# Query and key transposes moved from TensorE to the crossbar DMA from batch 3 on, with earlier loads, in a fused attention and mixer kernel

## The chip, the cores and the metric

One core of one Trainium2 chip. The metric is the device time of one execution in microseconds (us), lower is better. Times of one kernel on one chip mostly lie within 1%, with some executions over 1.5% above the fastest; those are called slow and left out of ratios, though not out of the medians. A ratio is the mean time of one kernel's fast runs over the mean of the kernel before's fast runs in the same rounds on the same chip, so it is not quite the ratio of the medians quoted beside it. The kernel before has medians from 400.4 to 406.0 us in the different rounds, so only ratios compare across rounds.

## The reference, cut to what matters

```python
# attention: B, H, S, D = 8, 8, 576, 64; q, k, v are 0.1 * randn, s is 0.5 * randn
scores = (1 / sqrt(D)) * q @ k.T                      # per head
cum    = cumsum(maximum(s, 0))
scores = where(causal, -1e9, scores + minimum(-(cum[:, None] - cum[None, :]), 0))
attn   = softmax(scores) @ v
# mixer on x = attention, heads side by side: [8, 576, 512]
u   = x + (x.T @ U @ V).T                             # rank 32, along the sequence
out = u + maximum(u @ w_ch1, 0) @ w_ch2               # 512 -> 2048 -> 512
```

## The kernel before: the parts that matter

The kernel works in pairs of heads: 32 pairs, four to a batch, numbered `n`. For a pair it needs q and k with the head dimension on the partitions ("slot"), and gets them by TensorE transposes into PSUM (the memory that TensorE's results land in) and VectorE copies out of it. Between the steps of attention (`run`), each `yield` lets a piece of the channel mixer (`fill`, four matmuls of 512 columns) go onto TensorE.

```python
def transposes(n):                       # pair n of batch b
    slot = slots[n % NSLOT]              # five slots
    ...                                  # rows of cum into the slot, by DMA
    for hh in range(2):
        tp = pwork()...                  # PSUM
        for c, src in enumerate((q_t[b], k_t[b])):
            for t2 in range(4):
                nc.tensor.transpose(tp[:, c, t2, :], src[:, h, ds(t2 * 128, 128)], identity[:TP, :TP])
        for par in range(2):
            copy(dst[:, :, :, :, par], tp[par * D : par * D + D]...)   # VectorE
        yield
...
load(2)
...
for n in range(PB, NP + 2):              # the second stage, pairs 4 to 31
    b, hp = divmod(n, PB)
    if hp == 0 and 1 < b < B - 1:
        load(b + 1)                      # q, k and v of the next batch, on GpSimd's queue
    if n + 1 < NP: run(transposes(n + 1))
    if n < NP:     run(scores(n))
    if hp == 1 and b > FT:
        run(seqmix(b - 1)); fill.append(chanmix(b - 1))
    if PB < n <= NP: run(values(n - 1))
    ...
in_program_order(tc, traced, [E.Pool, E.PE])
```

`values` ends in a VectorE division (a reciprocal and a multiply into `x_sb`) and a crossbar DMA (a DMA that transposes on its way) of `x_sb` into `xT`, which `seqmix` adds when it writes `uT`. The last line: in the second stage only GpSimd and TensorE run in the order of the program. The instructions of VectorE, ScalarE and SyncE are put in an order by the build tool, by when it expects each to be ready. VectorE then starts them in the order of its list: in the changed kernel below it sits idle 11.60 us in front of a copy while a reciprocal waits behind it.

The softmax here doesn't subtract the row's maximum and nothing guards it: scores larger than these inputs give would overflow.

## Time and profile before

| | before |
|---|---|
| median, first three runs | 404.92 us (401.1 to 407.01) |
| profiled execution | 403.4 us span, TensorE busy 95% |
| TensorE idle in a steady batch (182 to 223 us) | 0.28 of 41 us |
| period of a steady batch | 41.2 us |

The lines are in the prediction below. A line of the timeline gives start and duration in us, engine (PE is TensorE, DVE VectorE, ACT ScalarE, POOL GpSimd, SPq SyncE's queue), line of the program, operation, tile written and tile read, and in brackets the idle time before it and what ended that. A window row gives the busy us of each engine in that stretch. The period of a batch is the distance between the first matmuls of successive channel mixers (L442), which stand in the chain of waits at 184.22, 225.40 and 266.60 us.

### The profile page before, as it was taken

To read this page: it belongs to the slowest core of one execution; us is meant where nothing else is said; L and a number is where in the kernel's file an instruction comes from. 1 tells how busy PE (TensorE), PEld (TensorE's weight loads), DVE (VectorE), ACT (ScalarE), POOL (GpSimd) and SP (SyncE) were. 2 spreads that over 40 slices of the span, in tenths; PEclk is the share of its full clock that TensorE was granted. 3 is DMA by queue.
4 is the path that set the end of the run, shared out by engine and by line. 5 is a ranking of instruction groups with operands and counts; after the bars stand their busy time and mean duration, and the time that the engine had idled before them with its cause. 6 is when DMAs were issued, how large, how long until landed. Compare 5 with 4: busy or idle time off the path is not lost.

```text
span 403.4 us, 8541 instructions
## 1 busy us (share of the span) xinstructions
PE 382.8 (95%) x3525; PEld 218.2 (54%) x3525; DVE 223.3 (55%) x484; ACT 201.0 (50%) x384; POOL 56.3 (14%) x79
## 2 busy tenths in 40 slices
PE   7798998798999999999999999999999999999995
PEld 3575445465555556655555565555565554444442
DVE  7875124587756775667566856785678353002011
ACT  5552479551874358534853386328642930530710
POOL 5750023320230041003200230000000000000000
PEclk9758999999999999999999999999999999999999
DMA  5999999999399359837992599251224014301002
GB/s 76 169 211 207 151 93 102 134 151 105 61 153 111 73 97 137 79 72 112 147 80 72 100 151 70 63 122 21 19 70 120 18 34 130 80 18 69 19 26 79
DMA packets 94149, 38.33 MB, mean 95 GB/s; under 512 B 77150, under 2 KB 88446, under 8 KB 94110
## 3 DMA queue, kind: packets, MB, share of 16 engines
q0 software_dynamic: 53360, 18.44, 59.8%
q1 hardware_dynamic: 40750, 19.35, 26.7%
q8 instruction: 27, 0.44, 0.5%
q14 instruction: 12, 0.10, 0.1%
HBM read 37.51 MB, written 9.95 MB: 118 GB/s over the span
## 4 chain that ended last, share of the span: by engine, by line
PE 82%; DMA 10%; DVE 5%; POOL 1%; issue 1%; ACT 1%; DVEq 0%; ACTq 0%
PE pwork L454 29%; PE pwork L442 29%; PE pscore L260 10%; DMA k_sd<-in_k_dram 7%; PE pwork L323 6%; PE pwork L239 3%; DMA v_slot_102<-in_v_dram 2%; DVE o_sb L464 1%; PE pscore L151 1%; PE pwork L395 1%; DVE x_sb L333 1%; PE pwork L352 1%; DMA hT<-in_s_dram 1%; POOL v_slot_102 L193 1%; ACT pT_87 L271 0%
## 5 line engine op out<-in xcount | busy, mean ns | idle before, releaser
L454 PE MATMUL pwork<-w_sb,hT 128*128 128x512 bf16 x576 | 142.2, 381 | 0.2 <-ACT slot_96 L245 0.2
L442 PE MATMUL pwork<-uT,w_sb 128*128 128x512 bf16 x576 | 141.0, 379 | 0.6 <-ACT slot_96 L245 0.3
L449 ACT ACTIVATE hT<-pwork 128x512 bf16<-128x512 f32 x144 | 87.8, 609 | 107.7 <-PE pwork L442 107.1
L454 PEld LDWEIGHTS <-hT 128*128 128x128 bf16 x576 | 51.8, 98 | 49.1 <-issue 0.8
L442 PEld LDWEIGHTS <-w_sb 128*128 128x128 bf16 x576 | 50.6, 98 | 47.4 <-DVE uT L377 0.7
L464 DVE TENSOR_TENSOR o_sb<-pwork,u_sd 128x512 f32<-128x512 f32 x36 | 24.9, 692 | 63.8 <-PE pwork L454 62.6
L271 ACT ACTIVATE pT_87<-pscore 128x512 bf16<-128x512 f32 x32 | 19.3, 603 | 30.7 <-PE pscore L260 30.6
L333 DVE TENSOR_TENSOR x_sb<-pwork,rec 128x320 bf16<-128x320 f32 x64 | 31.3, 490 | 2.0
L271 ACT ACTIVATE pT_86<-pscore 128x512 bf16<-128x512 f32 x32 | 19.3, 603 | 19.5 <-PE pscore L260 19.4
L99 POOL DMA_DIRECT2D q_sd<-in_q_dram x10 | 8.1, 811 | 142.1 <-PE pwork L239 126.6
L245 DVE COPY slot_96<-pwork 64x576 bf16<-64x576 bf16 x22 | 17.4, 797 | 13.9 <-PE pwork L239 13.6
L272 DVE TENSOR_TENSOR pT_87<-pT_87,keep 128x512 bf16<-128x512 bf16 x32 | 13.2, 416 | 20.5 <-ACT pT_87 L271 20.5
L272 DVE TENSOR_TENSOR pT_86<-pT_86,keep 128x512 bf16<-128x512 bf16 x32 | 13.2, 414 | 18.5 <-ACT pT_86 L271 18.4
L239 PEld LDWEIGHTS <-q_sd 72*128 72x128 bf16 x256 | 16.3, 100 | 13.2 <-DMA q_sd<-in_q_dram 1.3
L239 PE MATMUL pwork<-identity,k_sd 72*128 72x72 bf16 x256 | 19.2, 201 | 4.2 <-DMA k_sd<-in_k_dram 4.2
L377 DVE TENSOR_TENSOR uT<-pwork,xT 128x256 bf16<-128x256 f32 (+6 forms) x54 | 19.4, 418 | 6.4 <-PE pwork L395 6.4
L323 PEld LDWEIGHTS <-pT_86 128*128 128x128 bf16 x480 | 19.0, 100 | 7.2 <-issue 2.0
L332 DVE RECIPROCAL rec<-pwork 128x5 f32<-128x5 f32 x64 | 12.2, 192 | 19.2 <-PE pwork L323 18.9
L284 ACT ACTIVATE pT_87<-pscore 128x512 bf16<-128x512 f32 x32 | 19.5, 610 | 6.2 <-PE pscore L260 6.2
L284 ACT ACTIVATE pT_86<-pscore 128x512 bf16<-128x512 f32 x32 | 19.5, 611 | 4.7 <-PE pscore L260 4.6
L245 DVE COPY slot_93<-pwork 64x576 bf16<-64x576 bf16 x26 | 20.6, 796 | 2.0 <-PE pwork L239 1.6
L323 PEld LDWEIGHTS <-pT_87 128*128 128x128 bf16 x480 | 18.8, 100 | 5.3 <-DVE pT_87 L297 0.3
(100 smaller groups left out, 441.3 us busy)
## 6 DMA issues: line engine op xcount, KB each, us to landing
out_dram<-o_sb SPq DMA_DIRECT2D x36, 256.0 KB
w_sb<-in_moe_w_ch_dram POOLq DMA_DIRECT2D x2, 2048.0 KB, 20.8
q_sd<-in_q_dram POOLq DMA_DIRECT2D x7, 576.0 KB, 8.4
k_sd<-in_k_dram POOLq DMA_DIRECT2D x7, 576.0 KB, 14.0
v_slot_102<-in_v_dram POOLq DMA_DIRECT2D x12, 128.0 KB, 13.5
v_slot_103<-in_v_dram POOLq DMA_DIRECT2D x12, 128.0 KB, 15.3
v_slot_104<-in_v_dram POOLq DMA_DIRECT2D x8, 128.0 KB, 17.6
rows_hbm<-hT SPq DMA_DIRECT2D x1, 504.0 KB
```

The lines of the kernel that those rows point to most:

```text
L239: nc.tensor.transpose(tp[:, c, t2, :], src[:, h, ds(t2 * 128, 128)], identity[:TP, :TP])
L245: copy(dst[:, :, :, :, par], tp[par * D : par * D + D].rearrange("p c t m -> p c m t"),)
L260: nc.tensor.matmul(dst, lhsT=kT[:, ds(j * 128, 128)], rhs=qT[:, lo:hi], start=True, stop=True,)
L271: nc.scalar.activation(pT[:, hh, 0:512], diag, EXP, scale=scale)
L272: nc.vector.tensor_tensor(pT[:, hh, 0:512].rearrange("p (a b) -> p a b", a=4), pT[:, hh, 0:512].rearrange("p (a b) -> p a b", a=4), keep.t ...
L284: nc.scalar.activation(pT[:, hh, 512:1024], far, EXP, scale=scale)
L323: nc.tensor.matmul(po[:, i, :], lhsT=pT[:, hh, ds(place(j, i), 128)], rhs=vt[:, j, h, :], start=(j == 0), stop=(j == i), skip_group_check= ...
L333: nc.vector.tensor_tensor(x_sb[:, hp, :, ds(hh * D, D)], po[:, :, 0:D], rec.to_broadcast([128, 5, D]), op=ALU.mult,)
L442: nc.tensor.matmul(f1, lhsT=w1_sb[:, kt, ds(nf * 128, 128)], rhs=u[:, kt, :], start=(kt == 0), stop=(kt == 3),)
L449: nc.scalar.activation(hT[:, nf, :], f1, RELU)
L454: nc.tensor.matmul(f2, lhsT=hT[:, nf, ds(i * 128, 128)], rhs=w2_sb[:, nf, :], start=(nf == 0), stop=(nf == NF - 1),)
L464: nc.vector.tensor_tensor(o_sb.rearrange("p (a b) -> p a b", a=4), f2.rearrange("p (a b) -> p a b", a=4), u_sd[:, :, i, :], op=ALU.add,)
```

## The change

Its intent: take 320 transposes off TensorE, which bounds the kernel, and let the DMA crossbar do them from batch 3 on, three pairs ahead. The q and k buffers become one tensor of 80 rows of which 72 are data, because the number of rows has to be a multiple of 16 (the prediction names the page); the spare eight are filled once by a DMA. The loads of q and k move two batches ahead.

```diff
+    qks = [consts.tile([TR, H, 2, TT * D], BF16, name=f"qk{i}") for i in range(2)]     # TR = 80
+    def fetch(n):
+        qkT_of[n] = work.tile([128, 2, 2, 4, TR], BF16, tag="qkT", name="qkT", bufs=3)
+        nc.sync.dma_start_transpose(out=qkT_of[n]..., in_=qks[b % 2][:, ds(2 * hp, 2), :, :]...)
     def transposes(n):
+        qkT = qkT_of.pop(n, None)
+            if qkT is not None:
+                tp = qkT[:, hh, :, :, :TP]           # the copies then read SBUF
+            else: ...                                # TensorE, as before
-        uxT = work.tile(..., tag="uxT")              # also ux
+        uxT = work.tile(..., tag="uxT", bufs=1)
...
-            load(b + 1)
+            load_v(b + 1)
+        nb = b + 2
+        if hp == (1 if b >= QT else 3) and QT <= nb < B:      # QT = 3
+            load_qk(nb, 0, H)
+        if hp == 1 and QT - 2 <= b < QT:
+            nc.sync.dma_start(out=qks[b % 2][TP:], in_=qks[b % 2][2 * TP - TR : TP])
+        if QT * PB <= n + 3 < NP:
+            fetch(n + 3)
```

More of the change, by code (lines that the diff above doesn't have):

```diff
@@ L70 @@
     FT = 2
+    QT = 3
     consts = ctx.enter_context(tc.tile_pool(name="consts", bufs=1))
-    loads = ctx.enter_context(tc.tile_pool(name="loads", bufs=2))
     work = ctx.enter_context(tc.tile_pool(name="work", bufs=2))
@@ L89 @@
     nc.sync.dma_start(out=s_sb, in_=s.rearrange("b h s -> (b h) s"))
-    q_t, k_t = {}, {}
-    def alloc_qk(b):
-        q_t[b] = loads.tile([TP, H, TT * D], BF16, tag="q_sd", name="q_sd")
-        k_t[b] = loads.tile([TP, H, TT * D], BF16, tag="k_sd", name="k_sd")
+    TR = 80
+    qks = [consts.tile([TR, H, 2, TT * D], BF16, name=f"qk{i}") for i in range(2)]
     def load_qk(b, h, n):
-        for dst, src in ((q_t[b], q), (k_t[b], k)):
+        for c, src in enumerate((q, k)):
             nc.gpsimd.dma_start(
-                out=dst[:, ds(h, n), :],
+                out=qks[b % 2][:TP, ds(h, n), c, :],
                 in_=src[b, ds(h, n)].rearrange("h (p t) d -> p h (t d)", p=TP),
             )
-    alloc_qk(0)
     load_qk(0, 0, 2)
@@ L169 @@
             )
-    for dst in (q_t[0], k_t[0]):
-        nc.vector.memset(dst[:, 4:8, 0:2], 0.0)
+    nc.vector.memset(qks[0][:TP, 4:8, :, 0:2], 0.0)
     load_qk(0, 4, 4)
@@ L210 @@
     nc.gpsimd.dma_start(out=w2_sb, in_=moe_w_ch2.rearrange("(kt kp) n -> kp kt n", kp=128))
-    alloc_qk(1)
     load_qk(1, 0, H)
     load_v(1)
-    uT_of, x_of, xT_of = {}, {}, {}
+    uT_of, x_of, xT_of, qkT_of = {}, {}, {}, {}
     def uT(g):
@@ L220, in uT @@
         return uT_of[g]
+    def fetch(n):
+        b, hp = divmod(n, PB)
+        qkT_of[n] = work.tile([128, 2, 2, 4, TR], BF16, tag="qkT", name="qkT", bufs=3)
+        nc.sync.dma_start_transpose(
+            out=qkT_of[n].rearrange("p a c t m -> p (a c t) m"),
+            in_=qks[b % 2][:, ds(2 * hp, 2), :, :].rearrange("p h c x -> p (h c x)"),
+        )
     def transposes(n):
@@ L231, in transposes @@
             )
+        qkT = qkT_of.pop(n, None)
         for hh in range(2):
             h = 2 * hp + hh
-            tp = pwork().bitcast(BF16)[:, : 2 * 4 * TP].rearrange(
-                "p (c t m) -> p c t m", c=2, t=4
-            )
-            for c, src in enumerate((q_t[b], k_t[b])):
-                for t2 in range(4):
-                    nc.tensor.transpose(
-                        tp[:, c, t2, :], src[:, h, ds(t2 * 128, 128)], identity[:TP, :TP]
-                    )
+            if qkT is not None:
+                tp = qkT[:, hh, :, :, :TP]
+            else:
+                tp = pwork().bitcast(BF16)[:, : 2 * 4 * TP].rearrange(
+                    "p (c t m) -> p c t m", c=2, t=4
+                )
+                for c in range(2):
+                    for t2 in range(4):
+                        nc.tensor.transpose(
+                            tp[:, c, t2, :],
+                            qks[b % 2][:TP, h, c, ds(t2 * 128, 128)],
+                            identity[:TP, :TP],
+                        )
             dst = slot[0:D, hh, 0 : 2 * S].rearrange("p (c m t two) -> p c m t two", c=2, t=4, two=2)
@@ L359, in seqmix @@
                 )
-        uxT = work.tile([128, 128], BF16, tag="uxT", name="uxT")
+        uxT = work.tile([128, 128], BF16, tag="uxT", name="uxT", bufs=1)
         nc.vector.tensor_copy(uxT, up)
@@ L365, in seqmix @@
         nc.tensor.matmul(up, lhsT=uxT, rhs=identity, start=True, stop=True)
-        ux = work.tile([128, 128], BF16, tag="ux", name="ux")
+        ux = work.tile([128, 128], BF16, tag="ux", name="ux", bufs=1)
         nc.vector.tensor_copy(ux, up)
@@ L516 @@
     in_program_order(tc, traced, [E.DVE, E.Activation, E.SP])
-    def load(b):
-        alloc_qk(b)
-        load_qk(b, 0, H)
-        load_v(b)
-    load(2)
+    load_qk(2, 0, H)
+    load_v(2)
     fill.append(chanmix(0))
```

## The prediction

> **What bounds the kernel now.** I read the views in this order: the page's busy shares and its forty slices, the table of windows, the timeline of TensorE inside one steady batch, then the DMA landings and the transposes on the queue of SyncE. First the page:
>
> ```profile
> PE 382.8 (95%) x3525; PEld 218.2 (54%) x3525; DVE 223.3 (55%) x484; ACT 201.0 (50%) x384; POOL 56.3 (14%) x79
> ...
> PE   7798998798999999999999999999999999999995
> ...
> PE 82%; DMA 10%; DVE 5%; POOL 1%; issue 1%; ACT 1%; DVEq 0%; ACTq 0%
> ```
>
> The reader should see that TensorE is busy 95% of the span and that the missing 5% lies in the first slices: from the tenth slice on every digit but the last is a 9. The chain of waits agrees, 82% TensorE. Its 10% of DMA are loads of the first three batches. The windows give it stage by stage (columns: busy of TensorE, weight loads, VectorE, ScalarE, GpSimd, then granted clock, DMA share, GB/s):
>
> ```profile
> 50.00:80.00 30.00, 25.67 (x267) 15.34 (x265) 12.80 (x28) 22.10 (x40) 8.61 (x13) 0.99 2.27 109
> 80.00:141.00 61.00, 58.57 (x634) 35.48 (x633) 43.87 (x93) 32.31 (x65) 8.99 (x11) 0.98 1.16 108
> ...
> 182.00:223.00 41.00, 40.72 (x414) 23.87 (x413) 27.91 (x59) 21.98 (x44) 5.88 (x7) 1.00 0.89 101
> ```
>
> In a steady batch (182 to 223 us) TensorE is idle 0.28 us of 41, at full clock; VectorE works 68% and ScalarE 54%. Only before about 98 us does anything else limit: there the DMA queues are overfull (share 2.27) and TensorE waits for q and k of batch 2. So what leaves TensorE's instruction stream after that shortens the run one for one, as long as nothing else makes TensorE wait.
>
> A busy time of pipelined matmuls overcounts, so I price a transpose by starts, not by durations. One half of a pair, inside a steady batch:
>
> ```profile
> 226.74 1.03 PE L442 MATMUL pwork<-uT,w_sb 128*128 128x512 bf16 x4
> 227.60 0.29 PE L239 MATMUL pwork<-identity,q_sd 72*128 72x72 bf16 x4
> 227.74 0.29 PE L239 MATMUL pwork<-identity,k_sd 72*128 72x72 bf16 x4
> 227.86 1.03 PE L442 MATMUL pwork<-uT,w_sb 128*128 128x512 bf16 x4
> 228.73 0.29 PE L239 MATMUL pwork<-identity,q_sd 72*128 72x72 bf16 x4
> ```
>
> Four channel-mixer matmuls hold the stream from 226.74 to 227.60, that is 0.86 us, and again from 227.86 to 228.73, 0.87 us. The eight transposes between them hold it 227.60 to 227.86, 0.26 us, or 32.5 ns each, although each is listed with a duration near 195 ns. The neighbours take the same time whether a transpose precedes them or not, so there is no hidden switching cost to win besides.
>
> **What the Trainium skill says.** "TensorE: Matmul & The Clock Gate", Part 4 (PE-mode transpose), gives about 390 ns for an isolated 128x128 transpose and about 275 ns in one kernel. The trace here disagrees as far as throughput goes: 32.5 ns from start to start, for 72 columns; priced at 275 ns the change would seem worth 88 us, and that is wrong for back-to-back transposes. "DMA: Bandwidth & Descriptors", DMA Transpose (X-bar), Constraints, asks for a partition dimension that is a multiple of 16; that is why the new buffers have 80 rows for the 72 used and why the spare eight are filled. The trace has no 80-row transpose; those it has are of 128 rows. "Advanced Engine Details and Errata", X-Bar Transpose (TRN2), expects 350 to 400 GB/s; the trace shows less, as worked out below. "Perfetto Trace Analysis", Optimizing Scalar/DVE Operations, puts the fixed cost of a VectorE operation at about 60 ns on SBUF and 125 ns on PSUM; the trace has no such copy from SBUF to compare.
>
> **The change part by part.** It removes the TensorE transposes of batches 3 to 7: 5 batches x 4 pairs x 16 = 320 instructions. In the trace those of pair 12, the first pair of batch 3, start at 115.8 us and the last end near 310.8. All lie in the saturated stretch. Cost: 40 groups of eight x 0.26 us = 10.4 us, all of it on the path. This is the main term.
>
> It adds 20 crossbar transposes on the queue of SyncE, each 80 rows x 2048 columns of 2 bytes = 0.33 MB. The existing ones:
>
> ```profile
> L340 SPq DMA_TRANSPOSE xT<-x_sb x24: 1199/1210/1776, 107.0 to 327.6; - x24
> ...
> L436 SPq DMA_TRANSPOSE u_sd<-uT x9: 1709/2009/8800, 43.7 to 344.9; - x9
> ...
> q1 hardware_dynamic: 672, 0.16, 14.2%
> ```
>
> The last line is a window of 6 us (318 to 324) that holds one xT transpose alone: 0.16 MB in 14.2% of 6 us = 0.85 us of all sixteen engines, 190 GB/s. A new transpose moves twice as much: 1.7 us alone, an estimate from that; 20 of them 34 us spread over some 190, a DMA share of 0.18 on top of the 0.89 of a steady batch, which already counts queueing twice, being the sum of two queues. SyncE's queue is held about 2 us by one of 2048 columns (the u_sd row), so 40 us over the same 190. Both fit. A loading burst of a steady batch lands thus:
>
> ```profile
> q_sd<-in_q_dram POOLq DMA_DIRECT2D x1, 576.0 KB, 7.9
> k_sd<-in_k_dram POOLq DMA_DIRECT2D x1, 576.0 KB, 13.2
> ```
>
> A transpose caught in such a burst may take 4 to 6 us instead of 1.7. It is asked for three pairs ahead, and a pair lasts about 8.9 us (transposes at 115.8, 124.7, 133.5), so it has about 18 us. Hidden. Loads of q and k start two batches ahead in the program; but in the trace GpSimd already issues batch 3's at 70.9 us and batch 4's at 108.6, as soon as the old buffer is free, so this part mostly keeps what there was now that the transposing DMA is the reader.
>
> It moves the copies into the slots (80 of them) from a PSUM source to an SBUF source:
>
> ```profile
> L245 DVE COPY slot_96<-pwork 64x576 bf16<-64x576 bf16 x22 | 17.4, 797 | 13.9 <-PE pwork L239 13.6
> ```
>
> They keep their stride-two destination, so I expect no faster mode: 797 ns less the skill's 65 ns is about 730 (estimate), 5 us of VectorE in all, off the path. Two PSUM buffers a pair come free, worth little with 0.28 us of idle a batch. Making uxT and ux single costs nothing, as their readers of the batch before are 39 us gone.
>
> Spare rows: two DMAs of 8 partitions x 16 KB = 131 KB. The first falls at about 64 us, in the overfull stretch where batch 2's k is on the path. 131 KB at that window's 109 GB/s is 1.2 us at worst; I take 0.4. With transposes gone, seqmix and the scores come sooner after the VectorE work they need: I take 0.02 to 0.03 us a pair or about 0.6 us. Sum: -10.4 + 0.4 + 0.6 = -9.4, so 404.9 - 9.4 = 395.5 us.
>
> **The rivals.** First, a wait takes the transposes' place: the copies now hang on a chain load, landing, crossbar, landing, copy, and VectorE takes its instructions in order. A copy placed early in its stream that waits for a late landing would hold back the masks and divisions behind it, and TensorE with them. For: the queue of SyncE already issues the slot rows four pairs ahead (the row for slot_95 at 192.03, just after that slot's last score), so the order is set by expected readiness, which may be too hopeful about DMA. Against: 18 us of lead and loads that land 13 us after issue. At 0.3 us a pair it gives back 6 us: about 400.
>
> Second, the crossbar traffic delays the xT transposes, which the sequence mixer adds at a batch's end. The last xT of a batch is issued at 213.21 and first read at 222.05; if a new transpose goes ahead of it, 2 us of queue plus up to 6 of data leave little of these 9. At 1 us in each of five batches: about 400.
>
> Third, VectorE becomes the bound: 27.9 us a batch against 41 - 2.1 = 38.9 leaves 11 us; I give it little. Fourth, TensorE was not really the bound and the time stays at 405: the 0.28 us of idle speaks against it. On the good side, if neither bubble nor spare-row cost appears it is 394.5, and with some of the 0.28 us a batch won besides, 393.
>
> **Range and chances.** The main term is firm (320 x 32.5 ns); the losses are the guess. Two per cent is 8.1 us, so the result is clearly faster only if the losses stay under 2.3 us. I put two in three on that, three in ten on a larger loss, and a twentieth on VectorE stalls that eat everything and more. Runs of the kernel before spread from 401.1 to 407.0, which widens the range: 391.5 to 401.
>
> **What would show it.** Right: L239's successor has 192 instructions left instead of 512; a steady batch lasts about 39 us with TensorE idle still under 0.5 us; the period of a pair falls by 0.52 us; the last stretch from the end of attention is the same 69 us; copies take about 730 ns with no long waits for a DMA. Wrong: VectorE waiting on DMA for qkT, TensorE waiting on VectorE slot copies or on uT, a batch period still near 41 us, or a start (to 98 us) longer by over 1 us.

## The result

The changed kernel takes 432.12 us (median of 4 runs, 430.08 to 435.64) against 405.97 us: ratio 1.0696, interval 1.0555 to 1.0838. It is 7% slower, where 2% faster was predicted (395.5 us, range 391.5 to 401). The page of its profile:

```profile
PE 381.4 (88%) x3205; PEld 210.0 (48%) x3205; DVE 211.3 (49%) x483; ACT 200.3 (46%) x384; POOL 57.5 (13%) x79
...
PE   8798988716799709899999999999999999999996
...
PE 58%; DMA 25%; issue 10%; DVE 5%; POOL 1%; ACT 0%; POOLq 0%; ACTq 0%; DVEq 0%; SPq 0%
```

The 320 transposes are gone (3525 to 3205 instructions), but TensorE's row now has two holes, a 1 near 90 us and a 0 near 155 us, and the chain is only 58% TensorE. By windows:

```profile
80.00:141.00 61.00, 44.50 (x415) 25.67 (x413) 37.55 (x76) 23.47 (x48) 11.69 (x14) 0.81 1.05 107
141.00:182.00 41.00, 25.12 (x220) 13.82 (x219) 19.03 (x45) 9.00 (x19) 5.87 (x7) 0.79 1.62 144
182.00:223.00 41.00, 40.54 (x366) 22.55 (x363) 26.13 (x61) 22.88 (x46) 6.61 (x7) 1.00 1.16 141
```

From 80 to 141 us TensorE was busy 58.57 us before and 44.50 now, and from 141 to 182 us it is busy only 25.12 of 41. The steady batch after that is fine. The starts of the second, third and fourth mixer tell the same story: 98.3, 143.1 and 184.2 us before, 119.7, 180.3 and 220.1 us now. So 21.4 us are lost by the first mark, another 15.8 to the second, and from there each of the next four batches gains 1.3 to 2.1 us. What TensorE waits for in the two holes:

```profile
87.76 0.43 PE L246 MATMUL pwork<-identity,qk_69 72*128 72x72 bf16 x8
101.44 0.66 PE L246 MATMUL pwork<-identity,qk_69 72*128 72x72 bf16 x8 [13.25 <-DVE x_sb L342]
101.90 1.90 PE L463 MATMUL pwork<-w_sb,hT 128*128 128x512 bf16 x4
103.60 0.69 PE L269 MATMUL pscore<-slot_92 68*128 68x128 bf16 x5
...
148.84 0.42 PE L269 MATMUL pscore<-slot_91 68*128 68x128 bf16 x5
163.63 1.87 PE L463 MATMUL pwork<-w_sb,hT 128*128 128x512 bf16 x4 [14.37 <-DVE x_sb L342]
```

Both times TensorE needs a PSUM buffer that VectorE has to divide out (`x_sb`), and VectorE comes late. After each hole the clock has dropped as well: four mixer matmuls take 1.70 us (101.90 to 103.60, at a granted clock of 0.50) where 0.86 is normal. That agrees with the Trainium skill, "TensorE: Matmul & The Clock Gate", Why this matters for your kernels, which warns of idle gaps over about 3 us between bursts of matmuls. And VectorE, in the same two places:

```profile
87.28 0.42 DVE L281 TENSOR_TENSOR pT_84<-pT_84,keep 128x512 bf16<-128x512 bf16 x1 [2.68 <-ACT pT_84 L280]
99.30 0.65 DVE L254 COPY slot_91<-qkT 64x576 bf16<-64x576 bf16 x1 [11.60 <-DMA qkT<-qk_70]
99.87 0.18 DVE L341 RECIPROCAL rec<-pwork 128x5 f32<-128x5 f32 x1
...
139.39 0.42 DVE L281 TENSOR_TENSOR pT_84<-pT_84,keep 128x512 bf16<-128x512 bf16 x1 [2.12 <-ACT pT_84 L280]
159.82 1.31 DVE L254 COPY slot_90<-qkT 64x576 bf16<-64x576 bf16 x2 [20.01 <-DMA qkT<-qk_69]
```

This is the key view. VectorE is idle 11.60 us and 20.01 us in front of a slot copy whose data the crossbar has not yet delivered, and the reciprocal that TensorE needs stands behind that copy. The copy at 99.30 is the first of pair 12, the first pair of batch 3. The reciprocal right behind it, at 99.87, is the thirteenth of the run; with two for a pair, it belongs to pair 6, and the program writes it four turns of the loop before that copy.

The copy's data did not come late for the program. Batch 3's k was issued at 77.26 us and landed at 93.86; SyncE had waited 12.0 us for it, and the crossbar transpose took another 5.4. In the kernel before, TensorE transposes this pair only at 115.8 us.

The second wait is the copy of pair 16, the first of batch 4, in front of the divisions of pair 10. Why its data was so late stands on GpSimd's queue and in the chain of waits of the changed kernel:

```profile
130.06 0.84 POOL L97 DMA_DIRECT2D qk_69<-in_q_dram  x1 [43.14 <-PE pwork L246]
130.90 0.82 POOL L97 DMA_DIRECT2D qk_69<-in_k_dram  x1
131.71 3.82 POOL L189 DMA_DIRECT2D v_slot_100<-in_v_dram  x4
135.51 0.70 POOL L193 DMA_DIRECT2D v_slot_100<-in_v_dram  x1
136.19 0.84 POOL L97 DMA_DIRECT2D qk_70<-in_q_dram  x1
```

```profile
130.90 11.49 DMA qk_69<-in_k_dram
142.44 17.30 DMA qkT<-qk_69
```

Batch 4's load waited for TensorE's transposes of batch 2, which the first hole had delayed from 108 to 130 us. Right behind it comes batch 5's load (qk_70 at 136.19; before, it was issued at 147.05). The crossbar transpose of pair 16 starts at 142.44, when batch 4's k has landed, and takes 17.3 us amid this burst.

### The profile page after: what moved, and what is told of

Same layout as the page of the kernel before. It is cut to its first block, busy times and chain, and to the rows that moved or that the text cites.

```text
span 433.6 us, 7969 instructions
## 1 busy us (share of the span) xinstructions
PE 381.4 (88%) x3205; PEld 210.0 (48%) x3205; DVE 211.3 (49%) x483; ACT 200.3 (46%) x384; POOL 57.5 (13%) x79
## 4 chain that ended last, share of the span: by engine, by line
PE 58%; DMA 25%; issue 10%; DVE 5%; POOL 1%; ACT 0%; POOLq 0%; ACTq 0%; DVEq 0%; SPq 0%
PE pwork L463 23%; PE pwork L451 23%; DMA qk_69<-in_k_dram 9%; DMA qk_70<-in_q_dram 7%; PE pscore L269 6%; PE pwork L332 5%; DMA qkT<-qk_69 4%; DMA qk_69<-qk_69 2%; DMA v_slot_99<-in_v_dram 2%; DVE o_sb L473 1%; PE pwork L404 1%; DVE slot_90 L254 1%; DMA hT<-in_s_dram 1%; POOL qk_69 L97 1%; POOL v_slot_99 L189 0%
## 5 line engine op out<-in xcount | busy, mean ns | idle before, releaser
L463 PE MATMUL pwork<-w_sb,hT 128*128 128x512 bf16 x576 | 145.7, 392 | 14.5 <-DVE x_sb L342 14.4
L451 PE MATMUL pwork<-uT,w_sb 128*128 128x512 bf16 x576 | 138.3, 380 | 0.6 <-ACT slot_93 L254 0.3
L463 PEld LDWEIGHTS <-hT 128*128 128x128 bf16 x576 | 54.4, 100 | 70.3 <-issue 19.9
L451 PEld LDWEIGHTS <-w_sb 128*128 128x128 bf16 x576 | 52.1, 98 | 51.9 <-issue 1.0
L280 ACT ACTIVATE pT_83<-pscore 128x512 bf16<-128x512 f32 x32 | 19.3, 604 | 32.9 <-PE pscore L269 32.8
L280 ACT ACTIVATE pT_84<-pscore 128x512 bf16<-128x512 f32 x32 | 19.3, 604 | 30.0 <-PE pscore L269 30.0
L293 ACT ACTIVATE pT_83<-pscore 128x512 bf16<-128x512 f32 x32 | 19.6, 612 | 21.3 <-PE pscore L269 21.2
L281 DVE TENSOR_TENSOR pT_83<-pT_83,keep 128x512 bf16<-128x512 bf16 x32 | 13.5, 421 | 32.5 <-ACT pT_83 L280 32.4
L246 PE MATMUL pwork<-identity,qk_69 72*128 72x72 bf16 x128 | 8.0, 214 | 17.3 <-DVE x_sb L342 13.2
L293 ACT ACTIVATE pT_84<-pscore 128x512 bf16<-128x512 f32 x32 | 19.6, 612 | 5.8 <-PE pscore L269 5.8
L254 DVE COPY slot_90<-qkT 64x576 bf16<-64x576 bf16 x16 | 10.5, 656 | 23.0 <-DMA qkT<-qk_69 20.0
L148 PE MATMUL pscore<-busy 128*128 128x512 bf16 (+1 forms) x53 | 20.4, 485 | 1.3 <-DVE busy L124 1.3
L297 ACT ACTIVATE pT_84<-pscore 128x512 bf16<-128x512 f32 x32 | 19.8, 619 | 0.0
L297 ACT ACTIVATE pT_83<-pscore 128x512 bf16<-128x512 f32 x32 | 19.8, 619 | 0.0
L254 DVE COPY slot_91<-qkT 64x576 bf16<-64x576 bf16 x16 | 10.7, 666 | 13.0 <-DMA qkT<-qk_70 11.6
```

Source lines behind the costliest of these rows:

```text
L254: copy(dst[:, :, :, :, par], tp[par * D : par * D + D].rearrange("p c t m -> p c m t"),)
L280: nc.scalar.activation(pT[:, hh, 0:512], diag, EXP, scale=scale)
L281: nc.vector.tensor_tensor(pT[:, hh, 0:512].rearrange("p (a b) -> p a b", a=4), pT[:, hh, 0:512].rearrange("p (a b) -> p a b", a=4), keep.t ...
L293: nc.scalar.activation(pT[:, hh, 512:1024], far, EXP, scale=scale)
L297: nc.scalar.activation(pT[:, hh, 1024:1536], mid, EXP, scale=scale)
L451: nc.tensor.matmul(f1, lhsT=w1_sb[:, kt, ds(nf * 128, 128)], rhs=u[:, kt, :], start=(kt == 0), stop=(kt == 3),)
```

## The experiments

Theory A after this reading: the wait is one of order. The build places slot copies up to four pairs early on VectorE, a late landing then blocks everything behind it. Rival B: the chain load, landing, crossbar, landing is too slow for the pace whoever waits. Rival C: the other parts (spare-row fill that holds SyncE until batch 2's k has landed, new places of the loads) start the loss. All kernels passed the comparison with the reference.

| run | median us | before us | ratio (95%) |
|---|---|---|---|
| e1 changed, VectorE in program order | 400.47 | 400.56 | 0.9973 (0.9946 to 0.9999) |
| e2 before, VectorE in program order | 406.71 | 400.56 | 1.0158 (1.0098 to 1.0218) |
| e3 changed, spare rows early | 434.31 | 400.56 | 1.0837 (1.0784 to 1.089) |
| e4 changed, no crossbar (faulty) | 424.29 | 400.56 | 1.0592 (1.0544 to 1.0639) |
| e5 no crossbar, loads late | 399.5 | 401.34 | 0.9897 (0.9809 to 0.9985) |
| e6 copies held | 400.77 | 401.34 | 0.989 (0.9774 to 1.0006) |
| e7 copies held, spare rows early | 403.1 | 401.34 | 0.9992 (0.9956 to 1.0028) |
| e8 no crossbar, dead crossbar traffic | 403.57 | 401.34 | 1.002 (0.9983 to 1.0056) |
| e9 copies held, loads after seqmix | 390.57 | 400.37 | 0.9746 (0.97 to 0.9792) |
| e10 changed, loads after seqmix | 456.15 | 400.37 | 1.133 (1.125 to 1.1409) |
| e11 = e6, beside e12 | 395.87 | 402.07 | 0.987 (0.9813 to 0.9928) |
| e12 = e9, beside e11 | 388.9 | 402.07 | 0.9704 (0.9652 to 0.9756) |

**e1 and e2: VectorE in program order, in the changed kernel and in the kernel before.**

```diff
-    in_program_order(tc, traced, [E.Pool, E.PE])
+    in_program_order(tc, traced, [E.Pool, E.PE, E.DVE])
```

> The changed kernel, with VectorE held to program order in the second stage, so that the slot copies of a pair stand right before that pair's scores and not up to four pairs ahead. Theory A (a copy placed early in VectorE's in-order stream waits for a late crossbar landing and holds back the divisions that TensorE needs; two such waits, 11.6 and 20.0 us, make the loss): both waits vanish, TensorE has no gap over 3 us after 80 us, the time falls from 432 to 395-400 us. Rival B (the chain load, landing, crossbar, landing is simply too slow for the pace, whoever waits): the wait moves to TensorE waiting on slot copies, time stays above 420. Rival C (SyncE blocked by the spare-row DMA, or the new load places): time stays near 430.

> Control: the kernel before, with the same hold of VectorE to program order. If the order alone is worth something, it shows here. Theory A expects nothing: there the copies wait for TensorE's transposes and stand next to them anyway; 403-408 us, ratio 0.99 to 1.01.

The two long waits are gone and 30 us with them, so theory A holds against B and C. But e1 misses its own numbers (400.47 us where 395 to 400 was expected, and a gap of TensorE of 3.86 us where none over 3 was): the time only draws level with the kernel before. Two reasons show. First, the control missed its expectation: program order by itself costs the kernel before 1.6%, with more waits of TensorE for `x_sb` before 92 us (0.98, 1.15 and 1.61 us, against one of 1.00 before). Against that control the crossbar is worth 0.9973 / 1.0158 = 0.982. Second, a new hole stands in e1's profile, TensorE first and VectorE second:

```profile
146.12 0.58 PE L451 MATMUL pwork<-uT,w_sb 128*128 128x512 bf16 x1 [3.86 <-DVE uT L386]
147.35 3.78 PE L451 MATMUL pwork<-uT,w_sb 128*128 128x512 bf16 x12
```

```profile
139.31 2.08 DVE L386 TENSOR_TENSOR uT<-pwork,xT 128x384 bf16<-128x384 f32 x6 [0.48 <-PE pwork L404]
145.51 1.09 DVE L386 TENSOR_TENSOR uT<-pwork,xT 128x384 bf16<-128x384 f32 x3 [4.13 <-DMA xT<-x_sb]
```

The last `xT` crossbar transpose of batch 2 was issued at 132.74 us and landed near 145.5, 12.8 us later. Batch 5's load had started at 130.50, which is likely the reason; e9 tests it. That is the prediction's second rival, at one batch.

**e3: spare rows filled from batch 1's rows,** so that SyncE does not wait 21 us for batch 2's k.

```diff
-        if hp == 1 and QT - 2 <= b < QT:
-            nc.sync.dma_start(out=qks[b % 2][TP:], in_=qks[b % 2][2 * TP - TR : TP])
+        if hp == 1 and b == 1:
+            for i in (1, 0):
+                nc.sync.dma_start(out=qks[i][TP:], in_=qks[1][2 * TP - TR : TP])
```

> The changed kernel with both spare-row fills taken from the first batch's rows in buffer 1, so that SyncE does not wait 21 us for batch 2's k before it can issue the second one. Theory A: the two waits of VectorE are set by the landings of batch 3's and batch 4's loads and by the order on VectorE, so the time stays within 425-434 us. Rival C (the fill blocks SyncE and that starts the loss): the first stall of 13 us goes and with it the second one's delay, time 405-418.

434.31 us: nothing gained, 0.3 us above theory A's range; the two holes of TensorE are still there (13.53 and 13.32 us). The fill blocks SyncE, but TensorE does not pay for it.

**e4: crossbar transposes left out (a faulty control).**

```diff
-        if QT * PB <= n + 3 < NP:
-            fetch(n + 3)
```

> The changed kernel with the crossbar transposes left out: TensorE transposes all pairs from the new joint q/k buffers; new load places, spare-row fills, single uxT and ux are kept. Theory A: all that is kept is harmless, 403-409 us, ratio 0.99 to 1.01. Rival C (new load places or fills cost the time): 412 us or more.

1.0592 looked like a point for rival C, and was my mistake. In the changed kernel the load of batch b+2 stands in the program after all four pairs of batch b have been fetched. Without the fetch it stands before TensorE's transposes of the last two pairs, which therefore wait for, and read, the wrong batch (in all, the times, the longest, in us):

```profile
PE pwork L246 <- DMA qk<-in_k_dram: 14.7, 5, 5.4
```

Its profile is of a slow run, so only this wait is read from it. The run says nothing of theory A. The wrong q and k passed the comparison. The likely reason, only argued, is that 0.1-sized q and k make scores of about 0.1 x 0.1 x 8 / 8 = 0.01, which barely count beside the bias. So passing here is weak evidence that a crossbar layout is right.

**e5 and e8: the mended control, and the same with crossbar traffic that nobody reads.**

```diff
-        if hp == (1 if b >= QT else 3) and QT <= nb < B:
+        if hp == 3 and QT <= nb < B:             # e5 and e8
-            fetch(n + 3)                         # e5: no fetch
-        qkT = qkT_of.pop(n, None)
+        qkT = None                               # e8: fetched, not used
```

> The control that the run without crossbar transposes was meant to be: there the loads of q and k still stood before TensorE's transposes of the batch they overwrite, so those waited for (and read) the wrong batch. Here the loads stand where all transposes of that batch are done (fourth pair). Joint buffers, spare-row fills, single uxT and ux kept, all transposes on TensorE. Theory A (nothing that is kept costs time): ratio 0.99 to 1.01. If the spare-row fill's hold of SyncE matters: up to 1.02.

> The control with all transposes on TensorE, and the 20 crossbar transposes issued besides, read by nobody: what their DMA traffic alone does. Theory A: within 1% of the control without them. If the traffic itself is the cost (late xT, late loads): 2% or more above the control.

e5 is at 0.990: joint buffers, fills and single `ux` cost nothing. e8 is at 1.002, 1.2% above e5 where theory A allowed 1%; by the ends of the intervals the traffic alone costs 0 to 2.5%. It is no 7%. The two profiled executions show no cost where the traffic flows: from the start of the second mixer (92.75 us in e5, 97.80 in e8) to the end both take 304.8 us. They differ before it, and e8's first crossbar transpose of q and k is issued only at 93.17.

**e6 and e7: only the copies held,** each behind the VectorE instruction that precedes it in the program, all else free; e7 with e3's spare rows besides.

```diff
+    def hold(at):                                # an order-only edge on VectorE
+        made = list(nc.cur_bb.bb.instructions)
+        prev = [i for i in made[:at] if i.engine == E.DVE][-1]
+        mine = [i for i in made[at:] if i.engine == E.DVE]
+        tc.add_manual_dep(mine[0], prev.name, DependencyInfo(NoSync, DATA), reason="hold")
...
+                at = len(nc.cur_bb.bb.instructions)
                 copy(dst[:, :, :, :, par], ...)
+                if qkT is not None:
+                    hold(at)
```

> The changed kernel with only the slot copies from the crossbar tiles held behind the VectorE instruction that precedes them in the program; all other VectorE work is free to be ordered as in the changed kernel. Theory A: both long waits of VectorE vanish and, unlike with all of VectorE in program order (which cost 1.6% in its control), nothing is paid for it: ratio 0.965 to 0.985. Rival B: ratio above 1.0.

> As the run before it, with both spare-row fills taken from batch 1's rows, so that SyncE doesn't wait for batch 2's k. If that wait costs TensorE anything in the first 100 us, this gains 1 to 3 us on the run before it; if not (as the equal starts to 80 us suggest), within 0.5% of it.

0.989 for e6 misses the 0.965 to 0.985 expected, though its interval reaches into it, and e7 at 0.9992 is outside the 0.5% expected (the spare rows early do not help; why this run is slower than e6 is not settled, and their intervals overlap). Neither profile has a wait of VectorE for `qkT`. Both again have TensorE holes behind a `uT` write that waits for `xT`, 0.98 us in e6 and 3.16 us in e7. The longest hole of e6 is another one, behind an output DMA that has not yet let go of its buffer:

```profile
184.85 0.71 PE L347 MATMUL pwork<-v_slot,pT 128*128 128x65 bf16 x15 [2.40 <-DVE o_sb L488]
```

```profile
184.11 0.69 DVE L488 TENSOR_TENSOR o_sb<-pwork,u_sd 128x512 f32<-128x512 f32 x1 [2.28 <-DMA out_dram<-o_sb]
```

Holding the copies removes the 30 us, and some later waits for DMA still eat part of the 10.4.

**e9 and e10: loads of q and k issued after the sequence mixer,** about when the kernel before issued them, with the copies held (e9) and not held (e10). GpSimd first reads a column of `uT`; it runs in the order of the program, so the loads follow.

```diff
-        if hp == (1 if b >= QT else 3) and QT <= nb < B:
+        if hp == 3 and b < QT and QT <= nb < B:
             load_qk(nb, 0, H)
...
             run(seqmix(b - 1))
+            if b >= QT and nb < B:
+                nc.gpsimd.tensor_copy(mark, uT_of[b][:, 3, 0:1])
+                load_qk(nb, 0, H)
```

> The copies held as in the run with only the copies held, and from batch 3 on the loads of q and k two batches ahead issued only after the sequence mixer of the batch before (GpSimd reads one column of its output first), where the kernel before issued them in effect. Theory D: with the stalls gone, what still eats the 10.4 us is that these loads now start about 15 us earlier, as soon as the crossbar has read the buffer, and their burst makes the last xT transpose of batch 2 land 12.8 us after its issue, so that TensorE waits 3.9 us near 146 us and runs slowly after it. Expected: no gap over 1 us near 146 us, ratio 0.970 to 0.982. If the gap stays or other waits take its place: 0.985 to 1.0.

> The changed kernel with the later loads alone, copies not held. The first long wait of VectorE (11.6 us, for batch 3's first pair) has nothing to do with these loads and stays; the second (20.0 us, for batch 4's first pair, whose crossbar transpose took 17.3 us beside two batches' loads) should shrink to about 8 us, as only its own batch's load must land. Expected: 415-424 us, ratio 1.03 to 1.06. If the second wait stays at 20 us, the burst was not what made that transpose slow.

e9 takes 390.57 us, ratio 0.9746: the gain that the transposes were priced at. Its page and its steady window:

```profile
PE 370.2 (96%) x3205; PEld 206.5 (53%) x3205; DVE 213.9 (55%) x483; ACT 200.7 (52%) x384; POOL 57.5 (15%) x82
```

```profile
182.00:223.00 41.00, 40.72 (x374) 23.09 (x373) 26.63 (x60) 23.91 (x49) 6.93 (x10) 1.00 1.27 140
```

TensorE idles 0.28 us in 41 again, as in the kernel before, and its mixers start at 175.3, 214.4 and 253.5 us: 39.1 us a batch against 41.2, the 2.1 us of 64 transposes. No gap of TensorE after 90 us exceeds 0.4 us. The last `xT` of batch 2 is issued at 127.50 us and nothing waits for it, although a crossbar transpose of q and k stands before it on SyncE's queue as in e1 (121.70 here, 126.81 there); batch 5's load now starts at 137.67. So the place on the queue alone does not make the wait.

e10 is a miss that teaches: expected 415 to 424, measured 456.15. The first wait stayed, as expected. The wait for pair 16 shrank (20.01 to 10.78 us, where about 8 was expected): with no second load beside it, its crossbar transpose took 8.3 us and not 17.3. But three more waits appeared:

```profile
101.76 0.64 DVE L254 COPY slot<-qkT 64x576 bf16<-64x576 bf16 x1 [12.79 <-DMA qkT<-qk]
153.89 1.31 DVE L254 COPY slot<-qkT 64x576 bf16<-64x576 bf16 x2 [10.78 <-DMA qkT<-qk]
196.40 0.66 DVE L254 COPY slot<-qkT 64x576 bf16<-64x576 bf16 x1 [11.06 <-DMA qkT<-qk]
245.79 1.30 DVE L254 COPY slot<-qkT 64x576 bf16<-64x576 bf16 x2 [8.16 <-DMA qkT<-qk]
294.73 1.99 DVE L254 COPY slot<-qkT 64x576 bf16<-64x576 bf16 x3 [8.24 <-DMA qkT<-qk]
```

I had forgotten that the copies of every batch stand early, and that in the changed kernel only the early loads hid this for batches 5 to 7. With loads where e9 has them, each batch's first copy blocks VectorE. The same load placement is good with the copies held and bad without: the order is the cause.

**e11 and e12: e6 and e9 again, on one chip and with five rounds,** as e6's interval was too wide to set beside e9's.

> The same kernel as the run with only the copies held, here on one chip with the next one, because its interval (0.977 to 1.001) was too wide to say what the place of the loads is worth by itself. Theory D: 4 to 7 us slower than the next one, ratio 0.985 to 0.995. If the loads' place is worth nothing: the two within 0.4% of each other.

> The same kernel as the run with the copies held and the loads after the sequence mixer, beside the one before it. Theory D: ratio 0.970 to 0.980, no gap of TensorE over 1 us after 100 us, a steady batch of 39.1 us against 41.2 us of the kernel before.

0.987 and 0.9704, intervals apart: the place of the loads is worth 1.7% once the copies are held. e12's profile has what was expected, steady batches of 39.0 to 39.1 us and no gap of TensorE over 0.4 us after 100 us.

How the place of the loads costs this time is not shown by these two profiles. e11's is of the fastest of its six runs (its four fast ones took 393.45 to 396.6 us) and has no hole near 140 us; e12's is of the slowest of its six (394.33; the others took 388.57 to 390.04). From the second mixer to the end the two take 294.5 and 294.3 us, the same. The collision of load and `xT` seems to happen in some executions and not in others: e1, e6 and e7 show it, e11's profile does not. That it slows the other runs of e11 is likely, and not shown.

The same measure helps with the other profiles, because what comes before the second mixer varies by itself: it starts at 98.29 us in the kernel before and at 92.75 in e5, neither of which has a crossbar transpose of q and k by then. From the second mixer to the end, the kernel before takes 305.1 us, the changed one 313.9, e1 300.7, e6 299.8, e7 300.9, and e9 294.3.

## Why the prediction was wrong

The main term was right. 40 groups of eight transposes at 0.26 us were priced at 10.4 us; e9 and e12 save 39.1 against 41.2 us a batch, ratios of 0.9746 and 0.9704 on 400 us are 10 to 12 us, and from the second mixer to the end both save 10.8 us. VectorE did not become the bound, the spare rows cost nothing measurable (e3), the joint buffers neither (e5).

The step that failed is "It is asked for three pairs ahead, and a pair lasts about 8.9 us [...], so it has about 18 us. Hidden." It counted the lead from the program's text, while VectorE's list is ordered by the build. There the copies stand up to four pairs earlier than in the program, which eats the whole lead. The first rival named just this, and quoted the evidence for it (slot rows issued four pairs ahead), but sized it as 0.3 us a pair spread evenly, about 400 us; VectorE stalls that eat everything got one chance in twenty. What came were two blocking waits of 11.6 and 20.0 us, TensorE holes of 13.25 and 14.37 us, and a halved clock after each. The two batch periods concerned grew by 21.3 and 15.8 us. With the copies held in place, both waits are gone (e1, e6). Each of the two waits was set by one late landing, so an average a pair was the wrong form of the term.

A second step failed by less: "so this part mostly keeps what there was". The load of batch 5 stands three turns of the loop earlier in the program, and the crossbar has read the buffer by then, so it was issued at 136.19 us in the changed kernel, and at 130.50 in e1, not at 147.05. It ran beside batch 4's load, and the crossbar transpose of pair 16 took 17.3 us where I allowed 4 to 6 (8.3 without it, in e10); in e1 the last `xT` was late beside it. That was the second rival's mechanism with another cause: I looked at new transposes going ahead of `xT` on SyncE's queue, what the profiles of e1 and e9 point to is a load under way at the same time (e11's profile has it without the wait). Its size, 1.7% between e11 and e12 (5.1 us between the means of their fast runs), is near the 5 us that I gave it.

Two smaller slips. The page's row of TensorE is 9 in every slice but the last from the eleventh on, not the tenth, which is an 8. And the copies were expected at about 730 ns and took about 657: the passage of "Perfetto Trace Analysis", Optimizing Scalar/DVE Operations, that puts PSUM and SBUF 65 ns apart adds that a profiled latency is about twice that, 130 ns apart (an estimate from it), and 797 to 657 ns, 140 ns, agrees.

What stays open: whether the crossbar traffic costs anything by itself (0 to 2.5% by the ratios, nothing in the profiled executions), what slows the other runs of e11, and why e7 was slower than e6.

## What to carry to other kernels

When a transfer takes the place of an engine's work, ask where the consuming instruction stands in its engine's real list, not in the program's text: the old copies, which depended on TensorE, caused no such wait, and the new ones, which depend on a DMA, were moved ahead of urgent work. (That the build expected the DMA too early is inferred from the order; its estimates were not looked at.) Hold such consumers to their place, and check what the earlier release of a buffer sets off, because the next load can start then and slow what is urgent (17.3 us for a crossbar transpose beside two loads, 8.3 beside one). The version that does both (e9, e12) beats the kernel before by 2.5 to 3%.

## What the Trainium skill lacked or had wrong

- "Advanced Engine Details and Errata", X-Bar Transpose (TRN2), expects 350 to 400 GB/s. A lone `xT` transpose of 0.16 MB ran at about 190 GB/s here (14.2% of 6 us of all sixteen engines, as the prediction works out). The section gives no rate for a transpose beside ordinary loads: the 0.33 MB transpose of pair 16 took 17.3 us beside two batches' loads.
- "TensorE: Matmul & The Clock Gate", Part 4, gives 275 to 390 ns as the time of one transpose and does not say how close together they can start. Back to back, 72-column ones started 32.5 ns apart here, each listed at about 195 ns, and removing 64 of them saved 2.1 us.
- No page that I found warns that a build can put a DMA's consumer ahead of urgent work in an engine's list: 11.6 and 20.0 us of idle VectorE in the changed kernel.
